# A fixed order for the Sync queue's DMAs, and three buffers for dV and dK, in the backward pass of a two-block attention kernel

## The chip, the cores and the metric

The kernel runs on one core of one Trainium2 chip. The metric is the time of one execution on the device, in microseconds (us). The kernel before takes 1765.45 us (median of three runs, 1764.07 to 1767.11). Profiles come from separate single executions; the span of the profiled one is a few us shorter than the timed runs (1763.2 us for the kernel before).

Engines: PE is TensorE, DVE is VectorE, ACT is ScalarE, POOL is GpSimd, SP is SyncE. "SPq" in a line of the profile is the Sync engine's sequencer, which here does nothing but issue DMAs. To evacuate is to copy a result from PSUM to SBUF; a DMA has landed when the last of its data has arrived.

## The reference

Two independent attention blocks, A and B, forward and all gradients. Cut to what matters:

```python
# per block: B, Sq, D = 8, 96, 640;  H, Sk, Dh = 32, 512, 128;  all bf16
q = (x @ wq).reshape(B, Sq, H, Dh).transpose(0, 2, 1, 3)
scores = einsum("bhqd,bhkd->bhqk", q, k_cache) * Dh ** -0.5
p = softmax(scores)
o = einsum("bhqk,bhkd->bhqd", p, v_cache)
out = o.transpose(0, 2, 1, 3).reshape(B, Sq, H * Dh) @ wo
# returned: both blocks' out, and the gradients of x, k_cache, v_cache, wq, wo of both, for a given grad_out
```

The large tensors are K and V, which are read, and dK and dV, which are written. K and V are needed in two layouts each: as stored (K for dQ, V for O) and transposed (K^T for S, V^T for dP).

## The kernel before

The unit of work is a tick: one head of one batch of one block. There are 2 x 32 x 8 = 512 ticks. In a tick PE makes S = Q K^T, the transpose of P, O, dP, dV, the transpose of dS, dK and dQ, each for another tick's data, so that the engines run as a pipeline. Work that belongs to a whole head (projections, dwq, dwo, and the sums for out and dx) is laid between the ticks. Between tick 224 and 288 the kernel changes from block A to block B: it loads and transposes block B's x and grad_out in column chunks while block A ends.

Heads go in pairs. For two ticks (a pair of heads, one batch) the Sync queue issues six DMAs of 256 KB each: K^T and V^T (transposing loads), K and V (plain loads), and the stores of dV and dK. Everything else (weights, x, grad_out, dwq, dwo, out, dx) is issued by POOL, but for block A's x and grad_out, which the Sync queue loads at the start.

```python
OFF = dict(t=-1, kn=3, vn=0, s2=3, s3=3, s4=4, s5=5, s6=6, s7=7, s8=8)
HP = 2
TB = 2
...
    def p_ldT(h, b, which):           # K^T or V^T of two heads
        def f():
            key = "KT" if which == 0 else "VT"
            t_ = kvp.tile([128, F4 * KC, 16], BF16, name=key + "_p", bufs=(4 if which == 0 else 6))
            src = (kc if which == 0 else vc)[b, h:h + HP].rearrange("h (r f) d -> (h r) (f d)", r=R8)
            nc.sync.dma_start_transpose(t_[:], src)
            ...
    def p_ldn(h, b, which):           # K or V of two heads
        def f():
            key = "K_sb" if which == 0 else "V_sb"
            t_ = kvp.tile([128, HP, KC, 128], BF16, name=key, bufs=4)
            src = (kc if which == 0 else vc)[b, h:h + HP]
            nc.sync.dma_start(t_[:].rearrange("p h c d -> p h (c d)"), src.rearrange("h (p c) d -> p h (c d)", c=KC))
            ...
    def p_st(h, b, which):            # store of dV or dK of two heads
        def f():
            t_ = CS[(blk, h, b)]["dV_p" if which == 1 else "dK_p"]
            dst = (dv if which == 1 else dk)[b, h:h + HP]
            nc.sync.dma_start(dst.rearrange("h (p c) d -> p h (c d)", c=KC), t_[:])
            ...
    def c_s4(h, b):                   # dV of one head; c_s7 does dK in the same way
        ...
            if j == 0:
                st["dV_p"] = wk.tile([128, HP, KC * 128], BF16, name="dV_sb", bufs=2)
            dV_p = CS[(blk, h - j, b)]["dV_p"]
            nc.scalar.activation(dV_p[:, j], dV_ps[:], ACT.Identity, scale=1.0)
...
                ob = wk.tile([128, w], BF16, name="ob", bufs=5)     # pieces of out and dx, stored by POOL
...
                if j == 0:            # where the six DMAs of a pair are put into the program
                    if b % TB == 0:
                        for which in (0, 1):
                            for bb in range(b, b + TB):
                                em.add(ct + OFF["t"], SLOTS["LOAD"] - 1, p_ldT(h, bb, which))
                    em.add(ct + OFF["kn"], SLOTS["LOAD"], p_ldn(h, b, 0))
                    em.add(ct + OFF["vn"], SLOTS["LOAD"], p_ldn(h, b, 1))
                    em.add(ct + HP + OFF["s4"], SLOTS["LOAD"], p_st(h, b, 1))
                    em.add(ct + HP + OFF["s7"] + 1, SLOTS["LOAD"], p_st(h, b, 0))
...
            stp=P(name="stp", bufs=3),                              # block B's x and grad_out chunks
```

These places are not the order on the queue. A scheduler orders each engine's instructions when the kernel is built. In the built kernel before, the Sync queue runs in a steady cycle **K, V^T, dV, K^T, V, dK**. It does not always keep to that cycle.

## Time and profile before

| | before |
|---|---|
| median time | 1765.45 us |
| profiled span | 1763.2 us |
| PE busy / idle | 1643.4 us (93%) / 119.8 us |
| mean granted PE clock | 0.984 |
| ACT's waits for the dK and dV stores | 47.8 us |

The page of the kernel before (busy us, share of the span, instructions; then what the DMA queues moved: packets, MB, share of 16 engines' span):

```profile
PE 1643.4 (93%) x22474; PEld 1371.8 (78%) x22648; DVE 1392.3 (79%) x3597; ACT 1349.2 (77%) x3529; POOL 712.9 (40%) x1306
...
DMA packets 320609, 458.39 MB, mean 260 GB/s; under 512 B 37216, under 2 KB 300896, under 8 KB 312128
...
q1 hardware_dynamic: 304672, 404.75, 87.7%
q0 software_dynamic: 15648, 49.83, 8.4%
```

PE is the busiest engine and its stream is what the kernel must follow. The DMA queues' packets fill 97% of the 16 engines' span, which looks like a second limit.

The waits of the kernel before (who waited, for what; us in all, times, the longest):

```profile
ACT dK_sb L428 <- DMA out_dram<-dK_sb: 24.5, 20, 3.3
...
ACT dV_sb L362 <- DMA out_dram<-dV_sb: 23.3, 16, 3.3
...
PE S_ps L286 <- ACT dK_sb L428: 18.1, 13, 3.3
...
DVE ob L521 <- DMA out_dram<-ob: 13.2, 11, 4.2
...
PE dV_ps L357 <- ACT dV_sb L362: 6.1, 5, 1.9
...
PE dK_ps L423 <- ACT dV_sb L362: 5.8, 7, 1.2
```

ACT evacuates dV and dK from PSUM into two SBUF buffers of each. In 36 cases it stands because a store has not yet emptied the buffer that it wants to fill. PE then stands for ACT. All PE waits of this kind, with smaller lines not shown, come to 36.9 us. The other large PE waits are for DVE (27.6 us, nearly all for dS) and belong to the pipeline itself.

The same view for the Sync queue, two of its lines:

```profile
SPq L246 <- PE o_ps L510: 120.1, 63, 3.6
SPq L246 <- PE dl_ps L383: 104.2, 66, 4.6
```

Line 246 is the transposing load. The lines of this view add up to 1268 us, so the queue seems to wait most of the time.

The timeline of the Sync queue of the kernel before, around its worst stall (start, duration of the issue):

```profile
1196.82 0.42 SPq L257 DMA_DIRECT2D K_sb<-in_B_k_cache_dram  x1
1197.33 1.15 SPq L246 DMA_TRANSPOSE VT_p<-in_B_v_cache_dram  x1
1198.58 0.53 SPq L266 DMA_DIRECT2D out_dram<-dV_sb  x1
1199.23 4.65 SPq L246 DMA_TRANSPOSE KT_p<-in_B_k_cache_dram  x1
1203.98 0.52 SPq L257 DMA_DIRECT2D V_sb<-in_B_v_cache_dram  x1
1204.91 0.38 SPq L266 DMA_DIRECT2D out_dram<-dK_sb  x1
...
1206.58 1.25 SPq L246 DMA_TRANSPOSE VT_p<-in_B_v_cache_dram  x1
1207.92 3.09 SPq L246 DMA_TRANSPOSE KT_p<-in_B_k_cache_dram  x1
```

and of ACT a little later (in brackets the idle time before, and what ended it):

```profile
1207.48 0.60 ACT L362 ACTIVATE dV_sb<-dV_ps 128x512 bf16<-128x512 f32 x1 [2.77 <-DMA out_dram<-dV_sb]
...
1210.64 0.60 ACT L428 ACTIVATE dK_sb<-dK_ps 128x512 bf16<-128x512 f32 x1 [1.89 <-DMA out_dram<-dK_sb]
```

The queue issues in order: the dK store at 1204.91 comes behind the 4.65 us K^T. The first of these ACT stalls is the dV store of 1198.58, which took until 1207.4 to land; the second is the dK store.

The records of the granted clock show PE at half clock for 3.4 or 6.8 us at 42.8, 77.0, 240.8, 834.7, 940.5, 998.6, 1104.4, 1210.2 and 1425.2 us, besides the kernel's end.

### The profile page before, as it was taken

To read this page: it belongs to the slowest core of one execution; us is meant where nothing else is said; L and a number is where in the kernel's file an instruction comes from. 1 tells how busy PE (TensorE), PEld (TensorE's weight loads), DVE (VectorE), ACT (ScalarE), POOL (GpSimd) and SP (SyncE) were. 2 spreads that over 40 slices of the span, in tenths; PEclk is the share of its full clock that TensorE was granted. 3 is DMA by queue.
4 is the path that set the end of the run, shared out by engine and by line. 5 is a ranking of instruction groups with operands and counts; after the bars stand their busy time and mean duration, and the time that the engine had idled before them with its cause. 6 is when DMAs were issued, how large, how long until landed. Compare 5 with 4: busy or idle time off the path is not lost. (4 is left out here: it accounts for less than half of the span.)

```text
span 1763.2 us, 59487 instructions
## 1 busy us (share of the span) xinstructions
PE 1643.4 (93%) x22474; PEld 1371.8 (78%) x22648; DVE 1392.3 (79%) x3597; ACT 1349.2 (77%) x3529; POOL 712.9 (40%) x1306
## 2 busy tenths in 40 slices
PE   5899989999999999998998999999999989999997
PEld 4787878788888888786886787877878878787776
DVE  4786868878888888887886778787888878888885
ACT  4888967878778787875876898786787867878782
POOL 3343434433433443434365344343443334343336
PEclk9899999999999999999999999999999999999999
DMA  9999999999999999999999999999999999999983
GB/s 267 262 280 258 265 251 262 270 261 273 266 266 284 264 268 257 273 271 259 242 278 282 262 268 273 249 268 252 264 265 269 262 239 265 267 269 246 263 249 111
DMA packets 320609, 458.39 MB, mean 260 GB/s; under 512 B 37216, under 2 KB 300896, under 8 KB 312128
## 3 DMA queue, kind: packets, MB, share of 16 engines
q1 hardware_dynamic: 304672, 404.75, 87.7%
q0 software_dynamic: 15648, 49.83, 8.4%
q8 instruction: 177, 2.90, 0.7%
q14 instruction: 112, 0.92, 0.1%
HBM read 161.09 MB, written 159.12 MB: 182 GB/s over the span
## 5 line engine op out<-in xcount | busy, mean ns | idle before, releaser
L298 ACT ACTIVATE E_sb<-S_ps,negm 96x512 bf16<-96x512 f32 x512 | 349.2, 682 | 212.6 <-DVE negm L288 203.6
L317 POOL TENSOR_SCALAR P_sb<-E_sb,rinv 96x512 bf16<-96x512 bf16 x512 | 354.2, 692 | 343.8 <-DVE rinv L308 339.4
L371 POOL TENSOR_TENSOR prod<-OT_h,dOT_h 128x96 bf16<-128x96 bf16 x512 | 188.1, 367 | 571.6 <-DVE OT_h L343 563.0
L385 DVE SCALAR_TENSOR_TENSOR dS_sb<-dP_ps,dl_ps,P_sb 96x512 bf16<-96x512 f32 x512 | 382.1, 746 | 35.4 <-PE dl_ps L383 22.4
L288 DVE TENSOR_REDUCE negm<-S_ps 96x1 f32<-96x512 f32 x512 | 347.9, 680 | 67.4 <-PE S_ps L286 66.6
L428 ACT ACTIVATE dK_sb<-dK_ps 128x512 bf16<-128x512 f32 x512 | 302.6, 591 | 108.9 <-PE dK_ps L423 70.4
L362 ACT ACTIVATE dV_sb<-dV_ps 128x512 bf16<-128x512 f32 x512 | 307.8, 601 | 26.0 <-DMA out_dram<-dV_sb 23.3
L346 ACT ACTIVATE PT_sb<-optp_ps 128x384 bf16<-128x384 bf16 x512 | 252.1, 492 | 0.9 <-PE optp_ps L340 0.5
L286 PE MATMUL S_ps<-KT_p,QT_h 128*96 128x512 bf16 x512 | 197.1, 385 | 18.6 <-ACT dK_sb L428 18.1
L357 PE MATMUL dV_ps<-dOnat_h,P_sb 96*128 96x128 bf16 x2048 | 200.4, 221 | 6.1 <-ACT dV_sb L362 6.1
L423 PE MATMUL dK_ps<-Qnat_h,dS_sb 96*128 96x128 bf16 x2048 | 199.9, 221 | 6.1 <-ACT dV_sb L362 5.8
L407 PE MATMUL dq_dst_ps<-ident,dS_sb 96*128 96x96 bf16 x2048 | 174.4, 208 | 27.9 <-DVE dS_sb L385 26.0
L381 PE MATMUL dP_ps<-VT_p,dOT_h 128*96 128x512 bf16 x512 | 197.3, 385 | 0.9 <-ACT dV_sb L362 0.9
L409 DVE COPY dST_sb<-dq_dst_ps 128x384 bf16<-128x384 bf16 x512 | 177.5, 347 | 15.3 <-PE dq_dst_ps L407 14.5
L333 PE MATMUL optp_ps<-PT_sb,V_sb 128*128 128x96 bf16 x2048 | 173.5, 207 | 5.2 <-ACT PT_sb L346 5.1
L340 PE MATMUL optp_ps<-ident,P_sb 96*128 96x96 bf16 x2048 | 173.4, 206 | 2.6 <-POOL P_sb L317 2.0
L400 PE MATMUL dq_dst_ps<-dST_sb,K_sb 128*128 128x96 bf16 x2048 | 172.9, 208 | 2.7 <-ACT dK_sb L428 2.5
L510 PE MATMUL o_ps<-wo_r,OT_h 128*128 128x256 bf16 (+1 forms) x1152 | 154.7, 259 | 1.4 <-ACT E_sb L298 0.3
L400 PEld LDWEIGHTS <-K_sb 128*128 128x128 bf16 x2048 | 135.9, 99 | 23.2 <-issue 3.6
L343 DVE CAST OT_h<-optp_ps 128x96 bf16<-128x96 f32 x512 | 126.8, 248 | 34.1 <-PE optp_ps L340 31.0
L510 PE MATMUL o_ps<-wqT_h,dQT_h 128*128 128x256 bf16 (+1 forms) x1152 | 150.4, 255 | 0.0
L308 DVE RECIPROCAL rinv<-rowsum 96x1 f32<-96x1 f32 x512 | 79.9, 156 | 87.5 <-ACT E_sb L298 65.8
(77 smaller groups left out, 3398.3 us busy)
## 6 DMA issues: line engine op xcount, KB each, us to landing
out_dram<-dV_sb SPq DMA_DIRECT2D x256, 256.0 KB, 4.1
out_dram<-dK_sb SPq DMA_DIRECT2D x256, 256.0 KB, 4.0
V_sb<-in_A_v_cache_dram SPq DMA_DIRECT2D x128, 256.0 KB, 4.0
K_sb<-in_A_k_cache_dram SPq DMA_DIRECT2D x128, 256.0 KB, 4.4
V_sb<-in_B_v_cache_dram SPq DMA_DIRECT2D x128, 256.0 KB, 4.0
K_sb<-in_B_k_cache_dram SPq DMA_DIRECT2D x128, 256.0 KB, 4.8
out_dram<-dwo_sb POOLq DMA_DIRECT2D x64, 160.0 KB, 5.0
out_dram<-dwq_sb POOLq DMA_DIRECT2D x32, 320.0 KB, 6.0
```

The costliest lines, as they stand in the source:

```text
L288: nc.vector.tensor_reduce(negm[:], S_ps[:], axis=AX.X, op=ALU.max, negate=True)
L298: nc.scalar.activation(E_sb[:].rearrange("q (a f) -> q a f", f=F4), st["S_ps"][:].rearrange("q (f a) -> q a f", f=F4), ACT.Exp, bias=st["n ...
L317: nc.gpsimd.tensor_scalar(P_sb[:], st["E_sb"][:], st["rinv"][:], 0.0, op0=ALU.mult, op1=ALU.add)
L346: nc.scalar.activation(PT_sb[:], PT_ps, ACT.Identity, scale=1.0)
L357: nc.tensor.matmul(dV_ps[:, c * 128:(c + 1) * 128], P_sb[:, c * 128:(c + 1) * 128], hs["dOnat_h"][:, b * 128:(b + 1) * 128], start=True, s ...
L362: nc.scalar.activation(dV_p[:, j], dV_ps[:], ACT.Identity, scale=1.0)
L381: nc.tensor.matmul(dP_ps[:], hs["dOT_h"][:, tok], st["VT"], start=True, stop=True)
L385: nc.vector.scalar_tensor_tensor(dS_sb[:].rearrange("q (a f) -> q a f", f=F4), dP_ps[:].rearrange("q (f a) -> q a f", f=F4), dl_ps[:, 0:1] ...
L400: nc.tensor.matmul(dQT_ps, st["K_sb"][:, c, :], st["dST_sb"][:, c * Sq:(c + 1) * Sq], start=(c == 0), stop=(c == KC - 1))
L423: nc.tensor.matmul(dK_ps[:, c * 128:(c + 1) * 128], dS_sb[:, c * 128:(c + 1) * 128], hs["Qnat_h"][:, b * 128:(b + 1) * 128], start=True, s ...
L428: nc.scalar.activation(dK_p[:, j], dK_ps[:], ACT.Identity, scale=1.0)
L510: nc.tensor.matmul(o_ps[:], src[:, t * 128:(t + 1) * 128], rhs, start=(hh == 0), stop=(hh == groups[g] - 1))
```

## The change

The intent: put the six Sync DMAs in a fixed order (K^T, V, dV on one tick, V^T, K, dK on the next), each placed two ticks or more behind the work that it waits for, so that none holds up those behind it; and give dV and dK a third buffer each. SBUF for that is taken from V^T (6 buffers to 4), `ob` (5 to 4) and block B's setup chunks (`stp`, 3 to 2).

```diff
-OFF = dict(t=-1, kn=3, vn=0, s2=3, s3=3, s4=4, s5=5, s6=6, s7=7, s8=8)
+OFF = dict(kt=-1, vt=2, vn=1, kn=4, dv=7, dk=10, s2=3, s3=3, s4=4, s5=5, s6=6, s7=7, s8=8)
-TB = 2
+class Chain:
+    def __init__(self, tc):
+        self.tc = tc
+        self.last = None
+    def __call__(self, res):
+        ins = getattr(res, "ins", res)
+        if self.last is not None:
+            self.tc.add_manual_dep(ins, self.last.name, mybir.DependencyInfo(mybir.DependencyClass.NoSync, mybir.DependencyReason.DATA), reason="issue order")
+        self.last = ins
+        return res
 ...
-  name=key + "_p", bufs=(4 if which == 0 else 6))
+  name=key + "_p", bufs=4)
-            nc.sync.dma_start_transpose(t_[:], src)
+            sp(nc.sync.dma_start_transpose(t_[:], src))          # and so for the other two kinds
-  name="dV_sb", bufs=2)
+  name="dV_sb", bufs=3)                                          # and so for dK_sb
-  name="ob", bufs=5)
+  name="ob", bufs=4)
-                    if b % TB == 0:
-                        for which in (0, 1):
-                            for bb in range(b, b + TB):
-                                em.add(ct + OFF["t"], SLOTS["LOAD"] - 1, p_ldT(h, bb, which))
-                    em.add(ct + OFF["kn"], SLOTS["LOAD"], p_ldn(h, b, 0))
-                    em.add(ct + OFF["vn"], SLOTS["LOAD"], p_ldn(h, b, 1))
-                    em.add(ct + HP + OFF["s4"], SLOTS["LOAD"], p_st(h, b, 1))
-                    em.add(ct + HP + OFF["s7"] + 1, SLOTS["LOAD"], p_st(h, b, 0))
+                    em.add(ct + OFF["kt"], SLOTS["LOAD"], p_ldT(h, b, 0))
+                    em.add(ct + OFF["vt"], SLOTS["LOAD"], p_ldT(h, b, 1))
+                    em.add(ct + OFF["vn"], SLOTS["LOAD"] + 0.1, p_ldn(h, b, 1))
+                    em.add(ct + OFF["kn"], SLOTS["LOAD"] + 0.1, p_ldn(h, b, 0))
+                    em.add(ct + OFF["dv"], SLOTS["LOAD"] + 0.2, p_st(h, b, 1))
+                    em.add(ct + OFF["dk"], SLOTS["LOAD"] + 0.2, p_st(h, b, 0))
 ...
-            stp=P(name="stp", bufs=3),
+            stp=P(name="stp", bufs=2),
+        pools["sp"] = Chain(tc)
```

The chain is an order among instructions of one engine; it adds no wait. PE's 45,298 rows stand exactly as before, DVE, ACT and POOL nearly so; the Sync queue runs **K^T, V, dV, V^T, K, dK**, always.

More of the change, by code (lines that the diff above doesn't have):

```diff
@@ L106, in build_block @@
     stp = pools["stp"]
+    sp = pools["sp"]
     def setup_ld(which_, c):
@@ L243, in f @@
             key = "KT" if which == 0 else "VT"
-            t_ = kvp.tile([128, F4 * KC, 16], BF16, name=key + "_p", bufs=(4 if which == 0 else 6))
+            t_ = kvp.tile([128, F4 * KC, 16], BF16, name=key + "_p", bufs=4)
             src = (kc if which == 0 else vc)[b, h:h + HP].rearrange("h (r f) d -> (h r) (f d)", r=R8)
-            nc.sync.dma_start_transpose(t_[:], src)
+            sp(nc.sync.dma_start_transpose(t_[:], src))
             for j in range(HP):
@@ L256, in f @@
             src = (kc if which == 0 else vc)[b, h:h + HP]
-            nc.sync.dma_start(t_[:].rearrange("p h c d -> p h (c d)"), src.rearrange("h (p c) d -> p h (c d)", c=KC))
+            sp(nc.sync.dma_start(t_[:].rearrange("p h c d -> p h (c d)"), src.rearrange("h (p c) d -> p h (c d)", c=KC)))
             for j in range(HP):
@@ L265, in f @@
             dst = (dv if which == 1 else dk)[b, h:h + HP]
-            nc.sync.dma_start(dst.rearrange("h (p c) d -> p h (c d)", c=KC), t_[:])
+            sp(nc.sync.dma_start(dst.rearrange("h (p c) d -> p h (c d)", c=KC), t_[:]))
             if which == 0:
@@ L359, in f @@
             if j == 0:
-                st["dV_p"] = wk.tile([128, HP, KC * 128], BF16, name="dV_sb", bufs=2)
+                st["dV_p"] = wk.tile([128, HP, KC * 128], BF16, name="dV_sb", bufs=3)
             dV_p = CS[(blk, h - j, b)]["dV_p"]
@@ L425, in f @@
             if j == 0:
-                st["dK_p"] = wk.tile([128, HP, KC * 128], BF16, name="dK_sb", bufs=2)
+                st["dK_p"] = wk.tile([128, HP, KC * 128], BF16, name="dK_sb", bufs=3)
             dK_p = CS[(blk, h - j, b)]["dK_p"]
@@ L511, in f @@
             if NG == 1:
-                ob = wk.tile([128, w], BF16, name="ob", bufs=5)
+                ob = wk.tile([128, w], BF16, name="ob", bufs=4)
                 evac(EV["gU"], ob[:], o_ps[:])
@@ L519, in f @@
             else:
-                ob = wk.tile([128, w], BF16, name="ob", bufs=5)
+                ob = wk.tile([128, w], BF16, name="ob", bufs=4)
                 nc.vector.tensor_tensor(ob[:], o_ps[:], acc[:, t, c0:c0 + w], op=ALU.add)
```

## The prediction

> **What bounds it now.** The page: PE 93% busy (1643 of 1763 us), DVE 79%, ACT 77%, DMA 97% of 16 engines' span. The chain of waits is nearly all PE. The start times of the 512 S matmuls show the pace: sixteen ticks (two heads, eight batches) take 48.8 us without group work and 55.3 us with it; others take 56 to 61.6 us. So PE's stream is the floor; stalls sit on top. DMA looks full but follows PE: four clean 32-tick periods in a row (about 530 to 840 us) took 104.1 to 105.5 us each, at about 270 GB/s (mean 260). DMA sustains that.
>
> **The stalls.** The waits view: ACT waits for the dK store 24.5 us (20 times) and the dV store 23.3 us (16 times). PE then waits for that ACT evacuation: S 18.1, dV 6.1, dK 5.8, K 2.5, others 4: about 36 of PE's 120 us idle. Timeline: at 1199.2 us the queue sits 4.65 us in a K^T transpose that waits for its buffer, then issues V, and only then the finished dK store; with two dK buffers ACT stands until 1210.6. The Trainium skill (DMA: Bandwidth & Descriptors, "Anatomy of one DMA") puts semaphore waits on the issuing sequencer, before dispatch; the queue's own waits agree (over 1,000 us). Second cost: the clock records show half clock for 3.4 to 6.8 us around such stalls (240.8, 998.6, 1104.4, 1210.2, 1425.2 us), 27 us, up to 13.6 us lost. The skill (TensorE: Matmul & The Clock Gate, Part 1) describes a gate driven by PE activity; the trace agrees.
>
> **What the change does.** The built order of PE is identical (45,298 rows), DVE and ACT nearly. Only the Sync order changes: one transpose, one load, one store per tick, strictly. Loads wait for a buffer freed 3 ticks earlier, stores for an evacuation 2 ticks earlier; the next write to a dV or dK buffer comes 3 ticks after the store's place, nominally 10 us, against 4.1 us to landing (longest 10.2). K^T, V^T, V, K have four ticks to land, 13 us against 5. ACT's waits for stores should fall from 48 us to under 8.
>
> **What it gives back.** Buffers: ob 5 to 4 (DVE already waits 13.2 us for ob stores) and block B's setup chunks 3 to 2. With two, each chunk load (6.0 us to landing) can start only after the transposes two chunks before; at 814 to 841 us PE already loses about 6 us there. I expect 4 to 8 us more there, 2 to 5 for ob. Waits for dS (26 us) and prod (5.5 us) stay.
>
> **Sum.** -36 (PE waits) -10 (clock) +8 (chunks, ob) = -38: **1727 us**, range 1708 to 1752. Cross-check: 16 periods at 104.1 save about 40 us. Chances: faster by over 2% 0.55, within 2% 0.43, slower 0.02.
>
> **What will show it.** No 58 to 61 us periods; ACT waits for stores near zero; PE's S idle under 5 us; mean clock about 0.99; half clock only at start, 835, 940 and end; DMA near 266 GB/s. Chunk and ob waits up.
>
> **What would make it wrong.** DMA being the real limit: then the packets' sum (1710 us) binds, and waits reappear as loads landing late. The strict order letting one late store hold up K^T. The block change costing 15 us or more, by holding up POOL's P and prod. Or waits on DVE taking the stalls' place.

## More of the kernel before

The issue times of block B's transposes in the kernel before (ns: shortest/median/longest):

```profile
L246 SPq DMA_TRANSPOSE KT_p<-in_B_k_cache_dram x128: 1095/2136/9622, 848.3 to 1704.4; - x128
...
L246 SPq DMA_TRANSPOSE VT_p<-in_B_v_cache_dram x128: 1095/1158/3212, 846.4 to 1702.2; - x128
```

K^T and V^T are the same transfer in shape and bytes, and their shortest issue is the same 1.095 us; but the median K^T takes nearly twice as long.

## The result

| | before | after |
|---|---|---|
| median time (range, four runs each) | 1766.28 (1764.07 to 1767.67) | 1710.81 (1708.59 to 1713.08) |
| ratio to before, 95% interval | 1 | 0.9687 (0.967 to 0.9704) |
| profiled span | 1763.2 | 1706.8 |
| PE idle | 119.8 | 72.9 |
| PE's waits for ACT's dV and dK evacuations | 36.9 | 0.4 |
| PE's waits for DVE / POOL | 27.6 / 7.5 | 28.0 / 6.9 |
| PE's waits for PT_sb of ACT | 5.1 | 0.8 |
| mean granted PE clock | 0.984 | 0.994 |

The ratios here are the mean time of one kernel's fast runs over the mean of the other's in the same rounds, so they are not quite the ratio of the medians. The change makes the kernel 3.1% faster; all outputs are right.

The page of the kernel after, its lines for the engines and the main DMA queue:

```profile
PE 1633.9 (96%) x22648; PEld 1359.3 (80%) x22648; DVE 1388.8 (81%) x3597; ACT 1345.0 (79%) x3529; POOL 713.3 (42%) x1306
...
DMA packets 320608, 458.38 MB, mean 269 GB/s; under 512 B 37217, under 2 KB 300897, under 8 KB 312129
...
q1 hardware_dynamic: 304672, 404.75, 91.3%
```

The same bytes are moved, faster, and PE's share rises from 93 to 96%. (The trace of before lacks 174 of PE's 22,648 matmul records, so that its busy time is a little too low and its idle time a little too high; the accounting below rests on start times and waits.)

The waits of the kernel after, the lines that answer to those shown of before:

```profile
DVE ob L536 <- DMA out_dram<-ob: 14.1, 16, 2.7
...
PE dl_ps L398 <- POOL prod L386: 5.2, 1, 5.2
...
ACT dK_sb L443 <- DMA out_dram<-dK_sb: 0.2, 1, 0.2
```

The store waits are gone: one of 0.2 us is left for dK, none for dV. The wait for `ob` is there as before, and one wait of 5.2 us for POOL stands out; it is taken up below.

The Sync queue of the kernel after, one steady cycle, and block B's transposes:

```profile
1151.15 1.56 SPq L261 DMA_TRANSPOSE VT_p<-in_B_v_cache_dram  x1
1152.76 0.57 SPq L272 DMA_DIRECT2D K_sb<-in_B_k_cache_dram  x1
1153.43 0.42 SPq L281 DMA_DIRECT2D out_dram<-dK_sb  x1
1153.94 1.17 SPq L261 DMA_TRANSPOSE KT_p<-in_B_k_cache_dram  x1
1155.21 0.53 SPq L272 DMA_DIRECT2D V_sb<-in_B_v_cache_dram  x1
1155.83 0.42 SPq L281 DMA_DIRECT2D out_dram<-dV_sb  x1
```

```profile
L261 SPq DMA_TRANSPOSE KT_p<-in_B_k_cache_dram x128: 1100/1320/4061, 821.1 to 1647.9; - x128
...
L261 SPq DMA_TRANSPOSE VT_p<-in_B_v_cache_dram x128: 1100/1324/4037, 831.1 to 1655.8; - x128
```

Two plain DMAs stand between any two transposes. The median K^T issue fell from 2.14 to 1.32 us; V^T rose from 1.16 to 1.32.

Where the time went, read from the start times of S matmuls (us; ticks count S matmuls):

| stretch | before | after | difference |
|---|---|---|---|
| start to the first S | 24.7 | 24.7 | 0 |
| ticks 0 to 32 | 93.3 | 83.3 | -10.0 |
| ticks 32 to 224 | 633.1 | 615.4 | -17.7 |
| ticks 224 to 288 (change of block) | 229.0 | 229.5 | +0.5 |
| ticks 288 to 480 | 643.2 | 614.5 | -28.7 |
| ticks 480 to 511 | 98.7 | 95.8 | -2.9 |
| last S to the end | 41.3 | 43.5 | +2.2 |

The three terms of the gain in the steady stretches: 36.5 us of PE's waits for dV and dK evacuations; half of 37.5 us, that is 18.7 us, because the stretches at half clock there shrank by 37.5 us; 4.3 us of waits for PT_sb. Together 59.5 us, and the steady stretches lost 59.3 us. This is an estimate, and the close fit is partly luck: 1.6 us of the 36.5 lie in the change of block, and PE stood idle for 4.2 of the 37.5 us at half clock, in which the clock cost nothing. Without these the terms come to 55.8 us, and 3.5 us stay unexplained. After the change, sixteen ticks take 48.8 and 53.8 us in turn with hardly an exception outside the change of block (which still has periods of 58.9 and 60.6), where the kernel before had 48.8 and anything from 55.3 to 61.6.

### The profile page after: what moved, and what is told of

The parts are those of the page before. It is cut to its first block, busy times and chain, and to the rows that moved or that the text cites. A ratio compares the mean times of both kernels' runs of the same rounds, so it can differ in the third digit from the quotient of the medians.

```text
span 1706.8 us, 59407 instructions
## 1 busy us (share of the span) xinstructions
PE 1633.9 (96%) x22648; PEld 1359.3 (80%) x22648; DVE 1388.8 (81%) x3597; ACT 1345.0 (79%) x3529; POOL 713.3 (42%) x1306
## 5 line engine op out<-in xcount | busy, mean ns | idle before, releaser
L400 DVE SCALAR_TENSOR_TENSOR dS_sb<-dP_ps,dl_ps,P_sb 96x512 bf16<-96x512 f32 x512 | 382.2, 746 | 30.0 <-PE dl_ps L398 17.7
L303 DVE TENSOR_REDUCE negm<-S_ps 96x1 f32<-96x512 f32 x512 | 347.9, 680 | 43.8 <-PE S_ps L301 42.8
L525 PE MATMUL o_ps<-wo_r,OT_h 128*128 128x256 bf16 (+1 forms) x1152 | 150.5, 254 | 1.4
L422 PEld LDWEIGHTS <-dS_sb 96*128 96x128 bf16 x2048 | 114.8, 98 | 33.7 <-DVE dS_sb L400 32.2
```

Of the source, the lines that this page charges most:

```text
L303: nc.vector.tensor_reduce(negm[:], S_ps[:], axis=AX.X, op=ALU.max, negate=True)
L400: nc.vector.scalar_tensor_tensor(dS_sb[:].rearrange("q (a f) -> q a f", f=F4), dP_ps[:].rearrange("q (f a) -> q a f", f=F4), dl_ps[:, 0:1] ...
L422: nc.tensor.transpose(dST_ps[:, c * Sq:(c + 1) * Sq], dS_sb[:, c * 128:(c + 1) * 128], ident[0:Sq, 0:Sq])
L525: nc.tensor.matmul(o_ps[:], src[:, t * 128:(t + 1) * 128], rhs, start=(hh == 0), stop=(hh == groups[g] - 1))
```

## The experiments

Twelve kernels were run, in three groups of four, each group on one chip: a_bufs2, b_bufs3, b_chain and a_nochain first; then a_grouped, a_half, b_kpool and a_extra; then the rest. A label that begins with a is the kernel after with an edit, one with b the kernel before. Theory Q has its present form from what the first group showed, and the second group was made to test it. The expectations also use letters B, C, D and F, each explained where it stands; R is the rival below. Theories:

- **Theory A**: the loss is ACT's wait for stores, and it comes from a store being held up on the queue, or from having only two buffers to ride it out. Then either half of the change alone, the order or the third buffer, should bring most of the gain.
- **Theory Q**: the Sync queue's own time to issue is nearly used up. How long a transpose takes to issue depends on what was issued just before it. The order makes the issues cheaper and so gives the queue slack; a third buffer alone gives none, because the stores simply fall further behind until the third buffer too is too few.
- **Rival**: the DMA engines, or the memory behind them, carry as much as they can, and the order only makes the data flow more smoothly.

To test Q we computed from each trace, for pairs 20 to 239, when each DMA's condition was met (for K^T: the end of the second S matmul of the pair four earlier, which frees its buffer; for a store: the end of ACT's second evacuation; and so on), and compared it with the start of its issue. "True wait" is the part of the time since the end of the previous issue in which the condition was not yet met. All columns are means or medians worked out by us from the traces, in us:

| kernel | median time | K^T, V^T issue | six issues of a pair | true wait per pair | lag of dV / dK store behind its evacuation (median) | ACT's waits for stores (whole run) |
|---|---|---|---|---|---|---|
| before | 1766 | 2.21, 1.29 | 5.59 | 0.63 | 1.7 / 2.3 | 47.8 |
| a_bufs2 | 1746 | 1.65, 1.48 | 5.27 | 0.88 | 0.0 / 1.1 | 25.5 |
| b_bufs3 | 1736 | 2.50, 1.32 | 5.99 | 0.07 | 6.3 / 7.2 | 35.9 |
| a_nochain | 1738 | 2.44, 1.32 | 5.90 | 0.14 | 5.9 / 6.7 | 23.5 |
| b_dk4 | 1733 | 2.53, 1.35 | 6.02 | 0.04 | 8.0 / 9.1 | 30.0 |
| a_grouped | 1742 | 2.26, 1.60 | 6.02 | 0.09 | 7.9 / 4.9 | 26.2 |
| b_chain | 1962 | 1.45, 1.44 | 5.03 | 2.04 | 0.0 / 3.6 | 205.2 |
| b_kpool | 1719 | 2.40, 1.30 | 5.25 (five) | 0.89 | 1.3 / 2.1 | 1.8 |
| a_extra | 1809 | 2.01, 1.47 | 6.28 (seven) | 0.04 | 8.4 / 8.6 | 88.4 |
| after | 1711 | 1.65, 1.52 | 5.36 | 0.64 | 0.4 / 1.3 | 0.2 |

Between two issues there are about 0.09 us more, 0.54 us for six. So for b_bufs3 a pair takes 5.99 + 0.07 + 0.54 = 6.60 us on the queue, of which 91% is issuing and nearly all the rest the gaps between issues.

The kernel before took 1765.66, 1765.56 and 1766.7 us (medians) on the three chips used; ratios below are to it.

### The order alone (a_bufs2)

```diff
 # the kernel after, with
-  name="dV_sb", bufs=3)
+  name="dV_sb", bufs=2)
-  name="dK_sb", bufs=3)
+  name="dK_sb", bufs=2)
```

> The changed kernel with dV and dK back in two buffers: the new order alone. Theory A (the gain is the end of ACT's waits for dV and dK stores; either an issue right after the evacuation or a third buffer is enough): the store is issued about when its evacuation ends and has some 10 us before the buffer is written again, against 4.5 us to landing, so ACT's waits for stores stay under 10 us (48 before, 0.2 after) and the time is 1708 to 1722. Theory B (the third buffer is what counts): ACT waits come back to 30 us or more, time 1745 or more. Theory C (the spacing of transposes makes DMA faster): same as after, 1711, but with transpose packets shorter than before's 1329 ns.

Measured: 1745.95 us (1738.36 to 1748.47), ratio 0.9874 (0.9816 to 0.9931). The line of its waits that matters:

```profile
ACT dK_sb L443 <- DMA out_dram<-dK_sb: 23.1, 21, 2.8
```

The waits for dV are all but gone (2.4 us), those for dK are as before. The median dK store follows its evacuation by 1.1 us, but one in ten by over 3.6 us, and landing takes 4.7 us in the median; with two buffers the next write comes 9.3 us after the evacuation, so the latest of them (up to 5.8 us of lag, and 5.4 us to landing in the stores that ACT stood for) don't make it. The order alone brings 20 us of 55. No theory had it right: A's time and wait are missed, B has the time (1745 or more) but not the wait (25.5 us, not 30). Theory C is out: a packet of a transpose (16 KB) takes 1.33 us in the kernel before, here and in the kernel after alike.

### The third buffers alone (b_bufs3)

```diff
 # the kernel before, with
-  name=key + "_p", bufs=(4 if which == 0 else 6))
+  name=key + "_p", bufs=4)
-  name="dV_sb", bufs=2)
+  name="dV_sb", bufs=3)
-  name="dK_sb", bufs=2)
+  name="dK_sb", bufs=3)
```

> The kernel before with dV and dK in three buffers (V^T buffers 6 to 4 to make room): buffers alone, the scheduler's order kept. Theory A: the longest wait for a store before was 3.3 us and a third buffer gives two more ticks (6.6 us), so ACT's waits for stores fall under 10 us and the time is 1712 to 1730. Theory D (the order counts: a queue standing at one transpose delays loads as well): the time stays above 1745. Theory C: no gain beyond 10 us.

Measured: 1735.6 us (1730.69 to 1740.92), ratio 0.9825 (0.9775 to 0.9875). Its waits for stores, and its K^T of block B:

```profile
ACT dK_sb L428 <- DMA out_dram<-dK_sb: 24.9, 23, 2.7
...
ACT dV_sb L362 <- DMA out_dram<-dV_sb: 11.0, 12, 1.7
```

```profile
L246 SPq DMA_TRANSPOSE KT_p<-in_B_k_cache_dram x128: 1095/2242/5505, 848.8 to 1679.2; - x128
```

With half as much buffer again, which puts the next write at 15.9 us after the evacuation in place of 9.5 (means), ACT still waits 23 times for dK. The stores are now issued 6 to 7 us after their evacuation, not 2. In the stores that ACT stood for, the lag was 10.3 us (dV) and 11.1 (dK) in the median and the landing 4.3 and 3.8, so that nearly all of it was used up. The queue has no true wait left (0.07 us per pair). Neither half brings the gain, and their gains (20 and 30 us) together fall short of the whole (55). Theory A, in the form "either half is enough", fell here; so did D, which had put the time above 1745.

### The chain at the old places (b_chain)

```diff
 # the kernel before, with the class Chain and sp(...) around the three kinds of Sync DMA; places and buffers as before
+        pools["sp"] = Chain(tc)
```

> The kernel before with its Sync DMAs chained in the order in which its own ticks emit them (dV V KT KT VT VT K dK dV V K dK), two buffers, V^T in six: a fixed order, but at the old places. Theory A: stores stand one tick behind their evacuation for dV, pairs of transposes ahead of others; ACT's waits for stores 20 to 60 us, time 1745 to 1790, so a fixed order by itself is not the gain. Rival (any fixed order is enough): within 10 us of 1711.

Measured: 1962.34 us (1957.72 to 1973.24), ratio 1.1117 (1.1058 to 1.1176). The queue now runs in the order that the old places spell out, dV, V, K^T, K^T, V^T, V^T, K, dK, dV, V, K, dK for two pairs.

```profile
ACT dK_sb L444 <- DMA out_dram<-dK_sb: 205.2, 75, 5.5
```

This is far outside every expectation. A fixed order is thus worth nothing by itself. Here the transposes issue fast (1.45 us) although four of them stand in a row, but the queue truly waits 2.04 us per pair for what isn't ready, and the dK stores stand behind it. What matters is which order, and that each DMA comes late enough to be ready.

### The places without the chain (a_nochain)

```diff
 # the kernel after, with
-        if self.last is not None:
+        if False:
```

> The changed kernel without the chain: new places, three buffers, the order left to the scheduler. As built its Sync order is nearly that of before (K VT dV KT V dK). Theory A: three buffers cover the late stores, so the same as b_bufs3, 1712 to 1730. Theory D: it stays above 1745 like before, because the order is before's.

Measured: 1738.26 us (1733.01 to 1743.48), ratio 0.9839 (0.979 to 0.9889). Without the chain the scheduler puts the queue back into K, V^T, dV, K^T, V, dK, as in the kernel before, and the kernel does what b_bufs3 does: K^T issues of 2.44 us, 0.14 us of true wait, stores 6 to 7 us late. Its K^T of block B, and its waits for dK:

```profile
L261 SPq DMA_TRANSPOSE KT_p<-in_B_k_cache_dram x128: 1095/2192/5122, 847.5 to 1680.4; - x128
```

```profile
ACT dK_sb L443 <- DMA out_dram<-dK_sb: 17.0, 15, 2.7
```

Theory A (1712 to 1730) and D (above 1745) both missed. The new places thus act only through the order, and the order is the difference between 1738 and 1711 us. This is the cleanest pair: places, buffers and bytes are the same, and only the order on the queue differs.

### Another fixed order: the transposes side by side (a_grouped)

```diff
 # the kernel after, with
-OFF = dict(kt=-1, vt=2, vn=1, kn=4, dv=7, dk=10, ...
+OFF = dict(kt=-1, vt=3, vn=1, kn=4, dv=8, dk=10, ...
```

The queue runs V, K, dK, dV, V^T, K^T. The chain, the three buffers and all bytes are as in the kernel after; the dV store and V^T stand one tick later.

> The changed kernel with the same chain and buffers, but the two transposes next to each other (V K dK dV VT KT). Theory A fell: neither half was enough. New theory Q: the Sync queue's own issue time binds; a K^T transpose issued right behind a V^T one takes 2.5 us to issue instead of 1.65, so the queue runs at its limit. Q expects here K^T issues of 2.3 us or more, K^T plus V^T 3.6 us or more a pair (3.2 after), stores issued 3 us or more after their evacuation in the median, and 1720 to 1745. Rival F (a fixed order and three buffers are enough, whichever order): 1706 to 1716.

Measured: 1741.86 us (1736.99 to 1748.92), ratio 0.9863 (0.9796 to 0.993). Its K^T issues and its store waits:

```profile
L261 SPq DMA_TRANSPOSE KT_p<-in_B_k_cache_dram x128: 1168/2194/4610, 847.4 to 1685.3; - x128
```

```profile
ACT dV_sb L377 <- DMA out_dram<-dV_sb: 26.2, 21, 3.4
```

With the chain and the buffers of the change, but the two transposes side by side, 31 of the 55 us are lost again. The issues sum to 6.02 us per pair and the queue has no true wait (0.09 us). Q's expectations held but for one by a hair (K^T 2.26 us, not 2.3), and F fell. The run is not clean, though: all of ACT's wait is for dV, and the dV store was moved one tick (some 3 us) later. The dK store, which kept its place, went from 1.3 to 4.9 us behind its evacuation, so the queue did fall behind; but with dV at its old place ACT might have waited less, and how much of the 31 us the order alone costs is not shown here.

Spacing, counted in DMAs, is not the whole cause either. Sorted by the number of plain DMAs between a K^T and the V^T before it, K^T took 2.59 us with none (65 cases) and 2.05 us with one (155) in the kernel before, and 1.65 us with two in the kernel after. But in b_bufs3 the same sorting gives 2.49 and 2.50 us, in b_chain transposes with none before them took 1.42 to 1.67 us, and in a_extra K^T took 2.01 us with two. What the traces show in its place stands under "Open" below.

### Half of the store's data (a_half)

```diff
 # the kernel after, with (in p_st)
-            dst = (dv if which == 1 else dk)[b, h:h + HP]
+            dst = (dv if which == 1 else dk)[b, h:h + 1]
-            sp(nc.sync.dma_start(dst.rearrange("h (p c) d -> p h (c d)", c=KC), t_[:]))
+            sp(nc.sync.dma_start(dst.rearrange("h (p c) d -> p h (c d)", c=KC), t_[:, 0:1]))
```

It leaves half of dK and dV unwritten; those outputs are wrong (NaN), the others right.

> The changed kernel storing only the first head of each dV and dK pair (wrong result on purpose: half of the gradients is not written), one sixth less data on the queue, the same number of DMAs. If the DMA engines' data rate still binds after the change (theory R): 1690 or less. If PE binds (Q and my prediction): 1700 to 1712. Q with back-pressure by data: transposes issue in under 1.35 us instead of 1.6; Q with a delay between transposes only: still 1.5 or more.

Measured: 1709.63 us (1706.16 to 1710.6), ratio 0.9671 (0.9621 to 0.9721).

```profile
DMA packets 255072, 391.27 MB, mean 229 GB/s; under 512 B 37217, under 2 KB 235361, under 8 KB 246593
```

A sixth of the queue's data is gone, the six issues take 4.77 us per pair, and the time is that of the kernel after (1710.81), with the same 48.8 and 53.8 us for sixteen ticks. So in the kernel after neither the DMA engines' data rate nor the queue's issue time sets the time of the steady stretches any more: PE's stream does. The rival is out for the kernel after. The transposes (1.36 and 1.27 us) fell between the two forms of Q in the expectation.

### K loads issued by POOL (b_kpool)

```diff
 # b_bufs3, with (in p_ldn)
-            nc.sync.dma_start(...)
+            (nc.gpsimd if which == 0 else nc.sync).dma_start(...)
```

Here the Sync queue keeps the scheduler's order but has five issues per pair in place of six; all bytes still move.

> b_bufs3 (the scheduler's order, three buffers) with the K loads issued from POOL: the same bytes, one DMA in six off the Sync queue. Q: the queue gets back some 0.5 us or more of each 6.6 us, stores are issued within 3 us of their evacuation (6 to 7 in b_bufs3), ACT's waits for stores fall from 36 us to under 12, time 1705 to 1724. R (data rate of the DMA engines): no relief, 1730 or more. POOL gets busier, which may cost up to 10 us.

Measured: 1718.59 us (1718.23 to 1720.0), ratio 0.9727 (0.9678 to 0.9777), 17 us less than b_bufs3 (on another chip, but the kernel before took the same on both, 1765.66 and 1765.56; the intervals of the two ratios just touch).

```profile
ACT dK_sb L428 <- DMA out_dram<-dK_sb: 1.8, 1, 1.8
```

The store waits go from 35.9 to 1.8 us with the same bytes moved and with K^T issues as long as ever (2.40 us). The queue gets 0.89 us of true wait per pair, which is slack, and the stores follow their evacuations by 1 to 2 us. The limit was the time of the issuing engine, not the DMA engines. The Trainium skill says this of the general case (Perfetto Trace Analysis, "DMA Optimizations"): if descriptor generation is the bottleneck, balancing DMAs over the engines that can issue them may help. This run agrees, with 17 us.

### One more load per pair (a_extra)

```diff
 # the kernel after, with (in p_ldn)
+            if which == 1:
+                x_ = kvp.tile([128, HP, KC, 128], BF16, name="V_again", bufs=1)
+                sp(nc.sync.dma_start(x_[:].rearrange("p h c d -> p h (c d)"), src.rearrange("h (p c) d -> p h (c d)", c=KC)))
```

> The changed kernel with each V load issued a second time into a spare tile: one DMA and 256 KB more in every two ticks. If the DMA engines have no spare rate (their share of the span says so), the queue needs 7/6 of the time: 1850 to 2000. If share of the span is no measure of fullness and there is a sixth to spare: under 1740. Q alone (0.6 us more issue a pair on 6.0): 1720 to 1800.

Measured: 1809.02 us, one run only, so that its state is unknown; outside all three expected ranges, 9 us above Q's.

```profile
DMA packets 390241, 525.52 MB, mean 291 GB/s; under 512 B 41312, under 2 KB 370528, under 8 KB 381760
...
q1 hardware_dynamic: 374304, 471.88, 95.1%
q0 software_dynamic: 15648, 49.83, 7.7%
```

```profile
ACT dK_sb L446 <- DMA out_dram<-dK_sb: 68.0, 47, 2.7
```

A seventh issue fills the queue (6.28 us of issues, 0.04 us of true wait), and the store waits are back at 88.4 us although dV and dK have three buffers and the good order. The DMA engines meanwhile move 291 GB/s, where the kernel before moved 260; the shares of the two main queues add up to 102.8% of 16 engines' span. So the kernel before, at 96.1% for the same two queues (97% with the small ones), was not at a limit of the DMA engines, and that share is no measure of how full they are. The Trainium skill warns of just this (Perfetto Trace Analysis, "Identifying the Most-Contended Engine": with 16 DMA engines, occupancy misleads).

### The kernel after once more, and with the buffers given back (after_again, a_ob5stp3, a_ob8stp3)

`after_again` is the kernel after, unchanged, run beside the next two on the same chip.

> The changed kernel itself, on the same chip as the next two, for comparison: 1708 to 1714.

Measured: 1711.26 us (1710.14 to 1713.79), ratio 0.9681 (0.9644 to 0.9718).

```diff
 # the kernel after, with
-                ob = wk.tile([128, w], BF16, name="ob", bufs=4)
+                ob = wk.tile([128, w], BF16, name="ob", bufs=5)      # a_ob5stp3;  bufs=8 in a_ob8stp3
-            stp=P(name="stp", bufs=2),
+            stp=P(name="stp", bufs=3),
```

> The changed kernel with ob back to 5 buffers and block B's setup chunks back to 3 (both still fit). It measures what these two reductions cost. My prediction put them at 8 us in sum: then 1701 to 1705. The traces of before and after suggest less: the stretch of the chunks took 27.0 us before and 26.5 after, the tail from the last S matmul 41.2 and 43.5, so 2 to 4 us: 1706 to 1709.

> The changed kernel with ob in 8 buffers and the chunks in 3. In the trace of after, at 908 to 912 us, DVE stands 2.7 and 1.1 us for an ob store (behind the bulk x and g loads), POOL's P and PE's dl wait behind it for 5.2 us, and the clock is at half for 6.8 and 3.4 us just then. If that reading is right, eight buffers end it and shorten the tail: DVE's waits for ob stores from 14 to under 5 us, the prod wait of 5.2 us gone, 1695 to 1704. If the 5.2 us come from POOL's own queue (the bulk load issue), it stays and the time is that of the run with 5 buffers.

Measured: a_ob5stp3 1702.49 us (1701.06 to 1707.84), ratio 0.9638 (0.96 to 0.9677); a_ob8stp3 1692.92 us (1689.48 to 1693.86), ratio 0.9571 (0.9534 to 0.9608). The waits for `ob`, and for `prod` of POOL, in after_again, in a_ob5stp3, and in a_ob8stp3, where DVE has no wait for a store of `ob` at all:

```profile
DVE ob L536 <- DMA out_dram<-ob: 17.3, 19, 5.3
...
PE dl_ps L398 <- POOL prod L386: 7.7, 1, 7.7
```

```profile
DVE ob L536 <- DMA out_dram<-ob: 10.8, 13, 3.7
...
PE dl_ps L398 <- POOL prod L386: 5.0, 1, 5.0
```

```profile
PE dl_ps L398 <- POOL prod L386: 1.3, 1, 1.3
```

Giving back what the change took from `ob` and the chunks is worth 8.8 us (1711.26 to 1702.49). Three more `ob` are worth another 9.6. The gain lies where it should: ticks 224 to 288 take 229.5 us in the kernel after, 222.2 with five, 215.6 with eight; the stretches before and after that agree to within 2 us, and the end is 43.5, 41.0 and 38.8 us. In the kernel after, at 908 us, DVE stands 2.71 and then 1.13 us for stores of `ob` that POOL issued at 902.4 and 902.9 us, behind the bulk load of block B's x (issued at 899.8, landed at 907.5), and that landed at 908.7 and 910.2; POOL's P and prod wait for DVE, and PE waits 5.2 us for prod; two stretches at half clock are close by (909.8 us, 6.8 us long, and 923.5, 3.4 long). a_ob8stp3 came out 2 us below its expected range, with 1.3 us of the wait for prod left; it is the best kernel.

### A fourth dK buffer in place of the order (b_dk4)

```diff
 # b_bufs3, with
-  name="dK_sb", bufs=3)
+  name="dK_sb", bufs=4)
-  name="ob", bufs=5)
+  name="ob", bufs=4)
```

> b_bufs3 with dK in four buffers (ob 4 to make room): can depth alone replace the order? Q: no. The queue in b_bufs3 waits for nothing (0.07 us a pair) and issues 90% of the time, so more depth only lets it fall further behind: dK stores issued 8 us or more after their evacuation, waits move to dV, 1726 to 1742. Rival (only the dK depth was short): 1718 or less.

Measured: 1733.32 us (1720.41 to 1742.18), ratio 0.9797 (0.974 to 0.9853).

The wait moved from dK to dV: no wait for dK stores is left, and those for dV rose from 11.0 to 30.0 us (23 times), with stores 8 to 9 us behind their evacuations. More buffer lets the backlog grow and moves the place where it shows; it doesn't shorten the queue.

## Why the prediction was right or wrong

The time was predicted as 1727 us (1708 to 1752) with "faster" the likeliest; it was 1710.81 us. The class and the range held; the point was 16 us too high. That the order helped as it did was in part luck. It put each DMA behind its condition so that the queue would wait less; but the queue's true wait is the same before and after (0.63 and 0.64 us per pair). What fell is the time to issue (5.59 to 5.36 us, at a faster pace), which the prediction doesn't name. Point by point:

**Right: the chain of stalls and its size.** "-36 (PE waits)" for the dV and dK evacuations: measured 36.9 to 0.4 us. ACT's waits for stores "under 8": 0.2. No other wait took their place: PE's waits for DVE stayed (27.6 to 28.0 us). The DMA rate was predicted at 266 GB/s and is 269, PE's idle before S under 5 us and is 0.4.

**Right: what is given back.** "+8 (chunks, ob)" is what a_ob5stp3 shows when it is taken away again: 8.8 us; how it divides between chunks and `ob`, no run tells. Between before and after only 2.7 us show (+0.5 us at the change of block and +2.2 at the end). What hid the rest is open: PE's store waits in the change of block were only 1.6 us before, and the half clock there is 13.7 us in both.

**Mis-sized: the clock.** The term "-10 (clock)" came out at 16.7 to 18.7 us (half of the time at half clock that went away, without and with PE's idle time in it). The prediction counted 27 us at half clock around five stalls and discounted that; it left out the start (42.8 and 77.0 us, 10.2 us long together) as not to be helped, and wrote "half clock only at start, 835, 940 and end". In the kernel after there is none at the start, and those that are left are three at the change of block and one at the end. But after_again, the same kernel, has 3.4 us at its start again (at 32.9 us), so that a part of this term varies from run to run. The stretches are all multiples of 3.4 us long, save the last one. The Trainium skill describes a gate that looks at free-running windows of about 3.4 us (TensorE: Matmul & The Clock Gate, Part 1); the traces agree with that length.

**Left out: PT_sb.** PE's waits for ACT's PT_sb fell from 5.1 to 0.8 us, as ACT was no longer late. Worth 4.3 us, not in the sum.

On paper these account for the miss: 8.7 us of clock (taken at 18.7), 4.3 of PT_sb, and 5.3 of give-back that was hidden (8 predicted, 2.7 net) make 18.3 us; the sum was predicted as -38 and was -56.4 us between the profiled spans. With what was said of the clock and of the give-back, some microseconds of it are not explained.

**The cross-check was a poor one.** "16 periods at 104.1 save about 40 us" took 32 ticks of the kernel before without a visible long stall for clean. The kernel after does 32 ticks in 102.6 us; the "clean" stretches still held short stalls (from 530 to 840 us, 4.3 us of PE's waits for ACT's dV and dK evacuations).

**Wrong: why the queue was late.** The prediction says that "the queue sits 4.65 us in a K^T transpose that waits for its buffer" and that the queue's own waits, over 1,000 us, agree. The buffer of that K^T was free at 1196.26 us, when the second S matmul of the pair four earlier ended; the issue began at 1199.23 us, three us later. It waited for no buffer; it took 4.65 us to issue. So it is throughout: no K^T issue in the kernel before began before its buffer was free. For 86% of them it was free before the queue had even ended the issue ahead, and so for 74 of the 81 that took over 2.5 us; the other seven had waited at most 0.19 us. True waits of the whole queue over 220 pairs come to 139 us, not over 1,000.

The waits view put the time down to waits because the semaphore that a transpose waits for is a counter of PE's progress that many instructions raise; the last raise that falls within the instruction's time on the queue is taken for its releaser, whether it was needed or not. That the names on the lines (`o_ps`, `dl_ps`) free no transpose's buffer should have been the warning. The Trainium skill has the rest (Perfetto Trace Analysis, "Per-instruction lifecycle", hardware-generated DMA): the profile's start of such an instruction is when its semaphores are satisfied, and what it shows is the wait for the descriptor generator and the generation itself. So 4.65 us of duration on the queue could not be a wait for a buffer, and this trace agrees: here the buffer had been free for 3 us, and in all 252 K^T issues that reuse a buffer the start comes after its release, by 0.03 us at the least. The same page ("What 'DMA-bound' means", second point) names the case: a kernel can be bound on the sequencer that issues, whose profiled time is descriptor generation and not data movement. The prediction looked for a bound in the DMA engines ("DMA being the real limit") and in waits, and not there. The passage that the prediction cites on waits is not at fault; the view of the trace was misread.

**So the mechanism that the runs support**: in the kernel before, a pair's six issues take 5.59 us plus 0.54 between them, of the 6.7 us that a pair has. When ACT and PE are given more room (a third buffer), PE runs faster, and the queue at 6.6 us per pair can't follow: stores fall back until the third buffer is used up (b_bufs3, a_nochain, b_dk4, a_grouped). The order of the change takes 0.6 us per pair out of that (5.99 to 5.36 us), mostly K^T. The queue then has slack, stores leave 0.4 to 1.3 us after their evacuation in the median, and the third buffer rides out the late tenth (4 to 5 us and more), which two buffers don't (a_bufs2). Both halves are needed for that reason. Taking an issue away by other means does nearly the same (b_kpool), adding one, with its data, undoes it (a_extra), and once the queue has slack, less data is worth nothing (a_half).

**Open.** What makes a transpose long to issue is not separated by an experiment. The kept traces point to the transpose before it. In the kernel before, a transpose took 1.21 us to issue when the one before it had landed or was within 2 us of landing, 1.68 us at 2 to 3 us before, 2.29 at 3 to 4, and 3.25 beyond (pairs 20 to 239). The kernel after gives 1.23, 1.60, 1.97 and 2.75, b_chain 1.22, 1.27, 1.73 and 2.28, a_extra 1.26, 1.76, 2.21 and 3.21. Of the 128 that took over 2 us in the kernel before, 121 ended before the earlier transpose had landed, by 1.0 us in the median (the K^T of 1199.23 by 0.8). This would also fit a_half, where transposes land sooner (4.7 us in the mean, 5.5 in the kernel after) and issue faster (1.36 and 1.27 us) in the same order. a_grouped fits less well (1.56 us in the first class), and a correlation is not a cause: no run tells a queue of descriptors that is full from a transposing unit that is busy.

## What to carry to other kernels

Add up, per period of the kernel, the time that each DMA queue spends issuing; if that comes near the period, the queue is a limit even though every single transfer is on time and the DMA engines could carry more, and more buffers only let the backlog grow. Cheaper issues (here by an order with two plain DMAs between any two transposes) or another issuing engine are then what helps, and a third buffer only after that. Before you believe that a queue waits, work out for a few instructions when their condition was truly met; and before taking buffers from elsewhere to pay for a change, look whether there is free memory: here that was worth 9 to 18 us.

## What the Trainium skill lacked or had wrong

- DMA: Bandwidth & Descriptors, "DMA Transpose (X-bar)", has no cost to issue for a transposing load of this size (elsewhere the page has one figure per instruction, for small tiles), and not that it depends on the transpose before. Here a 256 KB transposing load took at least 1.095 us of the Sync queue, against 0.4 to 0.7 us in the mean for a plain one; and in the kernel before 1.21 us in the mean when the transpose before it had less than 2 us left to its landing, 3.25 us when it had over 4.
- DMA: Bandwidth & Descriptors, "Issuing engines are not separate DMA queues", says that issuing on several engines saves only the sequencer's time to initiate, "which is usually small relative to the DMA itself". Small against one transfer (4 to 5 us to landing) it may be, but six in a row took 5.4 to 6.0 us of every 6.5 to 6.6 us here, and moving one of the six to POOL gained 17 us (b_bufs3 to b_kpool).
- No page says that the waits which a profile infers for a DMA queue can be wrong by most of their sum when the semaphore is a counter shared by all of an engine's instructions: 1268 us listed for the whole kernel, 139 us true over 220 of its 256 pairs.
